# Two score slots of three PSUM banks each, side work on one bank, two early passes, and a plan picked among forty

## The chip, the cores and the metric

The kernel runs on one core of one Trainium2 chip. The metric is the device time of one execution in microseconds (us). Times are medians; a ratio is the mean time of one kernel's runs over the mean time of the other's of the same rounds, so it is not quite the ratio of the medians.

## The reference

Two transformer layers with shared weights over 2048 tokens of width 512: attention with 32 heads of 16 columns, then a feed-forward block of 1792 columns.

```python
x = x + _A_ref(_layernorm(x), A_wqkv, A_wo)     # attention, scores * Dh ** -0.5, softmax
x = x + _B_ref(_layernorm(x), B_w1, B_b1, B_w2, B_b2)   # gelu(x w1 + b1) w2 + b2
x = x + _A_ref(_layernorm(x), A_wqkv, A_wo)
x = x + _B_ref(_layernorm(x), B_w1, B_b1, B_w2, B_b2)
```

The attention asks for 2 x 32 x 2048 x 2048 exponentials. They set the time.

## The kernel before

The kernel contains a planner. It walks all the work in Python, keeps a clock for each engine from assumed costs and hand-over times, places each operation greedily by readiness and priority, and emits one fixed instruction stream per engine with semaphores. On the chip nothing is decided any more. A constant that only enters the planner's clocks changes no instruction's work, only the order, and through the order also how many cells go to which engine.

A *cell* is one PSUM bank of scores: 128 keys by 512 queries; there are 4096. ScalarE turns the cells of a *slot* into exponentials, three or two banks in one instruction (a *turn*). VectorE makes some of the cells with an integer approximation. Of the eight banks, 0 to 2 and 3 to 4 are the two slots, 5 collects the products with V, 6 and 7 are side banks, into which PE writes *side units*: pieces of the projections and of the feed-forward, each of some 16 matmuls or a longer sum, read out by VectorE or ScalarE. Between them PE also runs *filler* matmuls, whose results nobody uses. In the cuts below `...` marks what is left out, and the comments are mine.

```python
SLOTS = ((0, 1, 2), (3, 4))
PVB = 5
MISC = (6, 7)          # side work: projections, feed-forward, output projection
EARLY = 4              # early passes of the second query block of layer 1
LATENCY = {"pe": 0.20, "act": 0.10, "dve": 0.10, "pool": 0.15, "sp": 0.1}
MM = 0.2135            # the planner's length of a group of matmuls
```

VectorE gets its cells in two ways. *Attach*: beside a turn's scores PE writes one more cell into a free side bank. *Swap*: the third bank of a slot goes to VectorE, and ScalarE's turn is cut to two banks. Such a slot is refilled only after both have read it.

```python
def swap(self, op, start, cells, extra, free):
    if extra or self.lend == 2 or len(cells) < 3 or not (self.open or self.s.pools["du"]):
        return
    if self.s.clock["dve"] > start + SWAP:      # VectorE would not get to it soon
        return
    ...
    cells.pop()
    ...
    self.join(op, d, SLOTS[0][2], extra, free)

def route(self, name, b):                       # where a freed side bank goes
    ...
    return "misc" if q > (0 if b == MISC[0] else QUEUE if ... else RUSH) or b == MISC[0] else "dbank"

def exps(self):                                 # ScalarE
    ...
    src = self.bank(SLOTS[sl][0], n).rearrange("p (j q) -> p j q", j=n)
    yield _Op("act", 0.065 + 0.4267 * n, lambda e, src=src, dst=dst: e.activation(
        out=dst, in_=src, func=ACT.Exp, scale=0.25), reads=..., writes=...)
```

A VectorE cell costs PE four products with V (V itself and three scaled copies), a ScalarE cell one.

The softmax here doesn't subtract the row's maximum and nothing guards it: scores larger than these inputs give would overflow.

## Time and profile before

| | before |
|---|---|
| median (6 runs beside the changed kernel) | 1588.74 us (1587.05 to 1592.41) |
| span of the profiled run | 1587.3 us |
| busy ScalarE / PE / VectorE | 97% / 90% / 85% |

The prediction below shows the lines of this profile and how they are read. One quantity needs a word. A turn of n banks keeps ScalarE for n x 426.7 + 51 ns from its start to the start of the next, if the next one's scores are there. Whatever passes beyond that between two successive exponentials I call the *lateness* of the second. I sum it over all successive pairs of the trace. In the profile's own rows most of it is hidden in the exponentials' durations, since a record can begin before the one before it has ended (two-bank records last at least 1017 ns and follow each other at 904 ns); only the longer gaps appear as idle time.

### The profile page before, as it was taken

The numbers are of one execution on the slowest core, as the hardware profiler recorded it, in microseconds if no ns is written. First come the engines' busy times: TensorE is split into PE (matmuls) and PEld (weight loads), VectorE is DVE, ScalarE is ACT, GpSimd is POOL, SyncE is SP. The second block draws the span as 40 slices with busy tenths as digits, with TensorE's granted clock in tenths as the row PEclk, the third lists the DMA queues.
The fourth block names the chain that finished last, engine by engine and source line by source line (L and its number), as shares of the span: only waits on it lengthen the run. The fifth ranks groups of instructions, "written<-read, shape, count | busy, mean of one in ns | idle before, by whom it ended". The sixth has DMA issues, their size and how long they took to land.

```text
span 1587.3 us, 42896 instructions
## 1 busy us (share of the span) xinstructions
PE 1424.2 (90%) x18701; PEld 444.6 (28%) x18701; DVE 1352.0 (85%) x2564; ACT 1547.1 (97%) x1393; POOL 200.5 (13%) x250
## 2 busy tenths in 40 slices
PE   8998888899999898988989998888998889898988
PEld 3222222222222222222222222222222222333344
DVE  5689999888898889978788789899878988998984
ACT  7999999999999999999999999999999999999996
POOL 5200012001100201002120020122001000010000
PEclk9999999999999999999999999999999999999999
DMA  5100001241114311143111510001251105312520
GB/s 140 22 2 1 2 14 41 77 132 46 27 45 130 85 41 28 42 140 74 36 28 48 172 44 28 1 2 33 67 167 43 28 15 151 103 36 87 155 82 29
DMA packets 141767, 96.88 MB, mean 61 GB/s; under 512 B 36877, under 2 KB 141582, under 8 KB 141582
## 3 DMA queue, kind: packets, MB, share of 16 engines
q1 hardware_dynamic: 141582, 94.14, 21.2%
q8 instruction: 149, 2.44, 0.6%
q14 instruction: 36, 0.29, 0.1%
HBM read 84.41 MB, written 2.10 MB: 55 GB/s over the span
## 4 chain that ended last, share of the span: by engine, by line
ACT 67%; PE 29%; DVE 2%; POOL 1%; issue 1%; DMA 0%; ACTq 0%; POOLq 0%
ACT pt L1466 60%; PE ps L512 11%; PE ps L1137 9%; PE ps L1527 8%; ACT g L893 3%; ACT v L1466 2%; ACT kt L1466 1%; ACT q L1466 1%; DVE du L1283 1%; ACT L893 1%; ACT L1466 0%; DMA xf<-xln 0%; PE ps L1125 0%; POOL xln L602 0%; POOL rstd L588 0%
## 5 line engine op out<-in xcount | busy, mean ns | idle before, releaser
L1466 ACT ACTIVATE pt<-ps 128x1536 bf16<-128x1536 f32 (+2 forms) x1261 | 1384.2, 1246 | 15.2 <-PE ps L1137 10.3
L1137 PE MATMUL ps<-qp,kt 32*128 32x512 bf16 x4096 | 538.0, 385 | 140.8 <-ACT pt L1466 106.7
L1283 DVE TENSOR_SCALAR du<-ps 128x512 uint16<-128x512 f32 x711 | 479.7, 685 | 97.5 <-PE ps L1137 89.6
L1527 PE MATMUL ps<-pt,v 128*17 128x512 bf16 (+1 forms) x3368 | 433.8, 359 | 2.3 <-ACT pt L1466 0.8
L1527 PE MATMUL ps<-du,vc 128*17 128x512 bf16 (+1 forms) x2394 | 333.8, 358 | 2.7 <-DVE du L1346 1.4
L1137 PEld LDWEIGHTS ps<-qp,kt 32*128 32x128 bf16 x4096 | 140.6, 91 | 685.9 <-ACT pt L1466 304.2
L1346 DVE TENSOR_SCALAR du<-du 128x2048 uint16<-128x2048 uint16 x361 | 246.3, 687 | 2.5
L1085 POOL TENSOR_SCALAR qp<-q,mask 128x512 bf16<-128x512 bf16 (+1 forms) x91 | 66.3, 728 | 1013.8 <-PE ps L1137 1005.1
L512 PE MATMUL ps<-xf,wr 128*32 128x512 bf16 (+1 forms) x2400 | 170.8, 368 | 1.7 <-DMA xf<-xln 1.1
L1527 PE MATMUL ps<-du,v 128*17 128x512 bf16 (+1 forms) x798 | 154.7, 360 | 1.7 <-DVE xt L743 0.9
L1344 DVE TENSOR_SCALAR du<-du 128x1024 uint16<-128x1024 uint16 x361 | 150.5, 428 | 2.0
L1527 PEld LDWEIGHTS ps<-pt,v 128*17 128x17 bf16 x3368 | 111.8, 89 | 113.0 <-issue 72.9
L512 PE MATMUL ps<-wr,g 128*32 128x512 bf16 x1600 | 123.8, 384 | 5.5 <-ACT g L893 5.0
L1527 PEld LDWEIGHTS ps<-du,vc 128*17 128x17 bf16 x2394 | 92.5, 89 | 62.7 <-issue 27.5
L872 DVE TENSOR_SCALAR g<-ps,hb1t 128x512 bf16<-128x512 f32 (+1 forms) x112 | 79.8, 713 | 13.8 <-PE ps L512 12.9
L1527 PE MATMUL ps<-dh,vc 128*17 128x512 bf16 (+1 forms) x321 | 90.6, 358 | 0.0
L1283 DVE TENSOR_SCALAR dh<-ps 128x512 uint16<-128x512 f32 x96 | 65.8, 685 | 11.5 <-PE ps L1137 10.8
L1283 DVE TENSOR_SCALAR kt<-ps 128x512 uint16<-128x512 f32 x82 | 56.1, 684 | 20.7 <-PE ps L1137 19.9
L512 PEld LDWEIGHTS ps<-xf,wr 128*32 128x32 bf16 x2400 | 53.6, 95 | 61.5 <-issue 33.5
L602 POOL TENSOR_SCALAR xln<-x,rstd,nmr 128x512 bf16<-128x512 bf16 x58 | 58.2, 1008 | 33.3 <-DMA xf<-xln 23.2
L754 POOL TENSOR_TENSOR ott<-xt,rc 128x256 bf16<-128x256 f32 x42 | 29.5, 703 | 178.5 <-DVE rc L746 178.5
L1125 PE MATMUL ps<-vc 128*32 128x512 bf16 x476 | 50.9, 395 | 0.1
(93 smaller groups left out, 1185.2 us busy)
## 6 DMA issues: line engine op xcount, KB each, us to landing
wr<-in_B_w_dram SPq DMA_DIRECT2D x256, 256.0 KB, 2.9
wr<-in_A_wqkv_dram SPq DMA_DIRECT2D x24, 256.0 KB, 2.9
wr<-in_A_wo_dram SPq DMA_DIRECT2D x18, 256.0 KB, 2.9
out_dram<-x SPq DMA_DIRECT2D x16, 128.0 KB, 2.7
g<-in_A_wqkv_dram SPq DMA_DIRECT2D x3, 512.0 KB, 5.1
x<-in_A_x_dram SPq DMA_DIRECT2D x3, 512.0 KB, 8.0
q<-in_B_w_dram SPq DMA_DIRECT2D x3, 512.0 KB, 3.9
kt<-in_B_w_dram SPq DMA_DIRECT2D x4, 256.0 KB, 3.3
```

The source lines that it names most:

```text
L512: return [lambda e, a=a: e.matmul(out[32 * a:32 * a + 32, :], lhsT=lhsT[:, 32 * a:32 * a + 32], rhs=rhs, start=start, stop=stop, tile_posi ...
L602: yield _Op(eng, cost, lambda e: e.tensor_scalar(T["XLN"][:, x, :], T["X"][:, t, :], T["RSTD"][:, t:t + 1], T["NMR"][:, t:t + 1], op0=ALU. ...
L872: yield _Op("dve", 0.21 + n / 966, lambda e, fc=fc, pb=pb: e.tensor_scalar(T["G"][:, fc, q], pb, T["HB1T"][:, fc:fc + 1], None, op0=ALU.ad ...
L893: lambda e, g=g: e.activation(out=g, in_=g, func=ACT.Gelu_apprx_tanh), reads=gk, writes=gk, prio=2)
L1085: yield _Op("pool", 0.1 + 0.6 * w / 512, lambda e, s=s, q=q, i=i, t=t, w=w: e.tensor_scalar(T["QP"][:, s, w * i:w * i + w], q, T["MASK"][: ...
L1125: fns.append(lambda e, o=o, w=w, a=a, m=m: e.matmul(o, lhsT=w, rhs=rhs, start=start, stop=start, tile_position=(0, m * a)))
L1137: return (lambda e: e.matmul(o, lhsT=lhsT, rhs=rhs, start=True, stop=True, tile_position=(32 * a, 0)), ["K%d.%d.%d" % (l, gb, kt // 4), "Q ...
L1283: yield _Op("dve", 0.68, lambda e: e.tensor_scalar(u, self.bank(b), E_SCALE, E_BIAS, op0=ALU.mult, op1=ALU.add), reads=["B.%d" % b], write ...
L1344: yield _Op("dve", 0.08 + 0.14 * n, lambda e: e.tensor_scalar(U[:, 1, 0:n, :], U[:, 0, 0:n, :], SHIFT, None, op0=ALU.add), reads=key[0], w ...
L1346: yield _Op("dve", 0.08 + 0.28 * n, lambda e: e.tensor_scalar(U[:, 2:4, 0:n, :], U[:, 0:2, 0:n, :], 2 * SHIFT, None, op0=ALU.add), reads=k ...
L1466: yield _Op("act", 0.065 + 0.4267 * n, lambda e, src=src, dst=dst: e.activation(out=dst, in_=src, func=ACT.Exp, scale=0.25), reads=["B.%d" ...
L1527: op.fns.append(lambda e, o=o, lhsT=q[0][0][m], rhs=q[0][1][:, n * m:n * m + n], a=a, st=st, sp=sp: e.matmul(o, lhsT=lhsT, rhs=rhs, start= ...
```

## The change

The intent is to widen ScalarE's turns. The second slot gets a third bank once the first layer's side work allows; side work then has bank 7 alone; a swap may cut either slot; the second query block has two early passes in layer 1; small hand-overs and priorities are set; and the constants of the planner are those of the best of forty draws by its own simulation.

```diff
-PVB = 5
-MISC = (6, 7)
+WIDE = 5
+PVB = 6
+MISC = (7, 5)
-EARLY = 4
+EARLY = 2
-LATENCY = {"pe": 0.20, "act": 0.10, "dve": 0.10, "pool": 0.15, "sp": 0.1}
+LATENCY = {"pe": 0.20, "act": 0.103924, "dve": 0.090771, "pool": 0.142879, "sp": 0.1}
-MM = 0.2135
+MM = 0.21347002580386326
@@ norm: explicit hand-over of the buffers XT and OTT
+        yield ("acq", "xt")
...
+        if ts[0] == 0:
+            yield ("take", ("ott", o))
@@ post: priority of the last layer norm
-            yield ("spawn", self.ln(ts, xf, xk, LNP, last), LNP)
+            yield ("spawn", self.ln(ts, xf, xk, LNP, last), 0.2 if last else LNP)
@@ route
+        if b == WIDE:
+            return "wide"
@@ vcopies, when the scaled copies of V are made
             self.lend = 1
+            if WIDE in self.s.pools["misc"]:
+                self.s.pools["misc"].remove(WIDE)
+                self.s.pools["wide"].append(WIDE)
@@ swap, in both slots
-        f, r = self.score(c, self.s.tokens[("qp", c[0])], SLOTS[0][2])
+        f, r = self.score(c, self.s.tokens[("qp", c[0])], self.slots[sl][2])
...
-        self.join(op, d, SLOTS[0][2], extra, free)
+        self.join(op, d, self.slots[sl][2], extra, free)
@@ dfirst
-        if b in MISC:
+        if b == MISC[0]:
             yield ("rel", "dbank", b)
         else:
-            yield from self.slot_done(0)
+            yield from self.slot_done(0 if b < 3 else 1)
+    def widen(self):
+        yield ("acq", "wide")
+        self.slots[1].append(WIDE)
... (the other lines replace SLOTS by self.slots, set up the new pools, and adapt
     the banks for filler matmuls and one condition on the last block)
```

More of the change, by code (lines that the diff above doesn't have):

```diff
@@ L737, in norm @@
         xt = T["XT"]
+        gb, ts = self.heads(seg, g)
+        yield ("acq", "xt")
         if part:
@@ L747, in norm @@
                   reads=["XT"], writes=["RC"])
-        gb, ts = self.heads(seg, g)
         o = gb % 2
+        if ts[0] == 0:
+            yield ("take", ("ott", o))
         pool = g < 6 and seg[2] == 512
@@ L757, in norm @@
                 reads=["XT", "RC"], writes=["OTT.%d.%d" % (o, t)])
+        yield ("rel", "xt", 0)
         if ts[-1] == 1:
@@ L761, in norm @@
                       writes=["OTN.%d.%d" % (gb, t % 4) for t in self.tiles(seg)])
+            yield ("rel", "ott", o)
             yield ("give", ("otn", l, seg, gb))
@@ L900, in ytile @@
         last = NFC // 2 - 1
-        for p in range(1 if (l, seg) == (NL - 1, self.segs[l][-1]) else NFC // 2):
+        for p in range(1 if tail else NFC // 2):
             yield ("need", ("g", l, seg, p))
@@ L1053, in setup_attention @@
         self.lead = [min(pi for pi, p in enumerate(self.pas) if p[0] == l) for l in range(NL)]
+        self.slots = [list(x) for x in SLOTS]
         self.held, self.users = [len(x) for x in SLOTS], [0] * len(SLOTS)
@@ L1093, in free @@
         src = self.source()
-        for b in (6, 7, 0, 1, 2, 3, 4, 5) if src else ():
+        for b in (7, 5, 0, 1, 2, 3, 4) if src else ():
             k = "B.%d" % b
@@ L1190, in join, with swap @@
         self.nd += 1
-    def swap(self, op, start, cells, extra, free):
+    def swap(self, op, start, cells, extra, free, sl):
         if extra or self.lend == 2 or len(cells) < 3 or not (self.open or self.s.pools["du"]):
@@ L1241, in scores @@
             cells = []
-            for _ in SLOTS[sl]:
+            for _ in self.slots[sl]:
                 c = self.next_act()
@@ L1248, in scores @@
                 break
-            work = list(zip(cells, SLOTS[sl]))
+            work = list(zip(cells, self.slots[sl]))
             fns, reads, writes, free, extra = [], [], [], [], []
@@ L1261, in scores @@
             op = _Op("pe", MM, fns, reads=reads, writes=writes, mode="S", slack=max(SLACK, ahead - LATE))
-            op.late = lambda op, start: (self.attach(op, start, cells, extra, free), self.swap(op, start, cells, extra, free))
+            op.late = lambda op, start, sl=sl, cells=cells, extra=extra, free=free: (self.attach(op, start, cells, extra, free), self.swap(op, start, cells, extra, free, sl))
             yield op
             self.held[sl] = len(cells)
-            self.users[sl] = 1 + any(e[1] in SLOTS[sl] for e in extra)
+            self.users[sl] = 1 + any(e[1] in self.slots[sl] for e in extra)
             for d, b, pair, j in extra:
@@ L1463, in exps @@
                 yield ("take", ("pt", r))
-            src = self.bank(SLOTS[sl][0], n).rearrange("p (j q) -> p j q", j=n)
+            src = self.bank(self.slots[sl][0], n).rearrange("p (j q) -> p j q", j=n)
             dst = self.unit(run)
@@ L1467, in exps @@
                 out=dst, in_=src, func=ACT.Exp, scale=0.25),
-                reads=["B.%d" % b for b in SLOTS[sl][:n]], writes=[k for r in run for k in self.pkeys(r)])
+                reads=["B.%d" % b for b in self.slots[sl][:n]], writes=[k for r in run for k in self.pkeys(r)])
             for r, (pi, kt, a) in zip(run, cells):
@@ L1478, in exps @@
             yield ("take", ("s", sl))
-            for b in SLOTS[sl]:
+            for b in self.slots[sl]:
                 yield ("rel", "misc", b)
@@ L1564, in run @@
         s.pool("dbank", [])
+        s.pool("wide", [])
+        s.pool("xt", [0])
+        s.pool("ott", [0, 1])
         s.route = self.route
@@ L1586, in run @@
         s.spawn(self.solo(), 4)
+        s.spawn(self.widen(), 4)
         for c in range(self.NQ):
```

## The prediction

> **What bounds the kernel now.** I read the page's first table, then its chain of work that ended last, then the groups by form on ScalarE and VectorE, then the waits, then the stretches of 40 us.
>
> ```profile
> PE 1424.2 (90%) x18701; PEld 444.6 (28%) x18701; DVE 1352.0 (85%) x2564; ACT 1547.1 (97%) x1393; POOL 200.5 (13%) x250
> ACT 67%; PE 29%; DVE 2%; POOL 1%; issue 1%; DMA 0%; ACTq 0%; POOLq 0%
> ```
>
> ScalarE is busy for 97% of the span and carries two thirds of the chain. Of its 40 us outside work, some 8 lie before 40 us and 15 after 1560 us, where the last feed-forward runs with no attention left. So between the ends ScalarE hardly ever stands still, and time is won there by giving it less to do, or by making its instructions follow each other more tightly.
>
> ```profile
> L1466 ACT ACTIVATE pt<-ps 128x1024 bf16<-128x1024 f32 x769 | 798.2, 1080 | 7.4 <-PE ps L1137 6.0
> L1466 ACT ACTIVATE pt<-ps 128x1536 bf16<-128x1536 f32 x491 | 740.2, 1507 | 7.8 <-PE ps L1137 4.2 <-PE ps L1527 1.3
> L1466 ACT ACTIVATE v<-ps 128x1536 bf16<-128x1536 f32 x18 | 26.6, 1477 | 0.2
> L1466 ACT ACTIVATE kt<-ps 128x1536 bf16<-128x1536 f32 x17 | 25.2, 1481 | 0.4 <-PE ps L1137 0.4
> L1283 DVE TENSOR_SCALAR du<-ps 128x512 uint16<-128x512 f32 x711 | 479.7, 685 | 97.5 <-PE ps L1137 89.6
> L1346 DVE TENSOR_SCALAR du<-du 128x2048 uint16<-128x2048 uint16 x350 | 241.2, 693 | 2.5
> L1344 DVE TENSOR_SCALAR du<-du 128x1024 uint16<-128x1024 uint16 x350 | 147.9, 433 | 2.0
> ```
>
> A cell of scores is one bank, 128 keys by 512 queries; there are 4096. ScalarE takes exponentials of three banks (1536 columns) or two (1024) at once, from the two slots in turn. Over all output names I count 540 instructions of three banks, 793 of two, one of one: 1334 instructions, 3207 cells, 2.40 cells each. VectorE makes the other 711 + 96 + 82 = 889 cells by its integer form; all its exponential groups sum to 1114 us, 1.253 us a cell, so its other work is 1352 - 1114 = 238 us. Equal slot turns would give 667 of each width; 540 means that 127 three-bank turns were cut to two by a swap that hands the third bank to VectorE. Then 762 of VectorE's cells came through the separate banks 6 and 7.
>
> From start to start the trace has a median of 904 ns after a two-bank exponential and 1331 ns after a three-bank one. The difference, 427 ns, is 512 columns at 1.2 GHz; what is left over either is 51 ns. Durations in the groups are longer because successive instructions overlap, so I use starts. Over all 1321 successive pairs of exponentials the excess over 427 ns a cell sums to 112 us: 67 us is the 51 ns floor, 45 us is lateness, and nearly all the lateness (41 us) follows two-bank instructions (mean excess over the floor 48 to 62 ns, against 7 ns after three banks).
>
> ```profile
> DVE du L1283 <- PE ps L1137: 89.6, 180, 3.1
> DVE kt L1283 <- PE ps L1137: 19.9, 22, 4.5
> DVE dh L1283 <- PE ps L1137: 10.8, 26, 2.1
> ```
>
> VectorE, which could relieve ScalarE, stands 120 us waiting for score cells, half of its 235 us of idle time. The stretches show where:
>
> ```profile
> 160.00:200.00 40.00, 32.41 (x364) 8.74 (x363) 37.77 (x74) 39.99 (x36) 3.02 (x4) 1.00 0.01 2
> 680.00:720.00 40.00, 35.78 (x470) 11.00 (x470) 27.63 (x50) 39.88 (x32) 1.34 (x3) 1.00 0.53 154
> 880.00:920.00 40.00, 36.72 (x483) 10.88 (x485) 30.17 (x53) 39.80 (x37) 1.39 (x2) 1.00 0.55 158
> ```
>
> The columns after the stretch's length are busy PE, weight loads, VectorE, ScalarE, GpSimd, then clock and DMA. With no side work (160 to 200 us) VectorE is 94% busy. In the second feed-forward product (high DMA) it falls to 69 to 75%, while ScalarE stays full: both side banks are held for long sums, and cells reach VectorE only by a swap in the one three-bank slot.
>
> **What the Trainium skill says.** "Perfetto Trace Analysis", section "Optimizing Scalar/DVE Operations", gives about 51 ns of access overhead per ScalarE instruction on PSUM and advises grouping when the engine is saturated. The start-to-start medians above agree to the nanosecond. The same page, "Identifying the Most-Contended Engine", takes occupancy as a fair measure for ScalarE and VectorE but not for matmuls; so 90% of PE is no proof that PE is close behind, and PE also runs 476 + 468 matmuls (L1125) of pure filler, 95 us of busy records. "PSUM — Partial Sum Buffer", section "PSUM bank collisions raise a hardware error", asks for semaphores by bank: a three-bank slot of which one bank goes to VectorE may only be refilled when both readers are done. This trace shows the cost of such waits as the lateness above.
>
> **The change part by part.**
>
> 1. Slots (0,1,2) and (3,4) become (0,1,2) and (3,4,5) once the first layer's projections are nearly done. Bank 5 is a side bank until then, so the opening keeps two side banks and 3 + 2. If no turn were swapped, 3207 cells would take 1069 instructions, a gain of 265 x 51 ns = 13.5 us. But every swapped turn drops back to two.
>
> 2. Afterwards side work has bank 7 alone, and VectorE's separate cells may use it only when no side unit holds it. A projection, first-product or output-projection unit is 0.98 us of matmuls (chain rows) plus a VectorE read of 0.69 to 0.75 us and two hand-overs: I estimate 2.5 us as interleaved. Four wo, fourteen first-product and twelve projection units make 75 us per segment of 192 us; four long sums of sixty matmuls at about 7 us make 28. So bank 7 is held some 54% of the time. It fits, but about half of the cells that came by separate banks must now come by swap.
>
> 3. Swaps are allowed in both slots. With about 450 of the cells swapped and 470 attached, ScalarE's width is about 2.6: from 3 x N = 3175 + 450 comes N = 1208 and a width of 2.63; I take 2.6, N = 1221. Saved: 113 x 51 ns = 5.8 us.
>
> 4. More cells for VectorE: up to one swap offer per turn instead of one per two turns, just where both side banks were busy. I assume that a third of its 120 us of score waits is recovered: 40 us / 1.253 us = 32 cells, 921 in all. Each spares ScalarE 0.427 us: 13.7 us. The ceiling is 1024 cells (4 of 16 key tiles), and the first 75 us offer hardly any, so a large leap is not possible.
>
> 5. Lateness: about 60% of turns now have three banks. 733 x 7 ns + 488 x 60 ns = 34 us against 45. Swapped slots wait for VectorE as well, so I take 9 us less, not 11.
>
> 6. Two early passes instead of four: two partial copies (0.69 us) and two adds (0.68 us) fewer, 2.7 us of VectorE, about 2 cells, under 1 us of time. It leaves 480 instead of 576 cells to cover the last segment's side work of layer 0, which is paced over 450. It should just fit.
>
> 7. The transposed-output buffers get explicit hand-over and the last normalization a higher priority. The tail of 26 us after the last exponential is one chain through PE (L512, 14 us in one piece); I give it 1 us. Changed latency constants alter no instruction; they shuffle the plan and, with a pick of forty by the planner's own clock, promise perhaps more than the chip will give. I count nothing.
>
> 8. Cost: side units can no longer overlap one's product with another's evacuation. Where a chain of them sets when a segment's next stage starts, ScalarE may run dry: 4 us, mainly at the layer boundary (1040 to 1160 us, where ScalarE already lacks 3.4 us in two stretches).
>
> Sum: -5.8 - 13.7 - 9 - 1 - 1 + 4 = -26.5 us, counted as -26: 1589.7 - 26 = **1564 us**, 1.6% less.
>
> **The rivals.**
>
> A. The swaps eat the width. If side work holds bank 7 more than I think, nearly all VectorE cells come by swap: N = (3207 + 889)/3 = 1365, more instructions than now, so no width gain; only lateness and the tail move: about 1580 to 1588. For it: 127 swaps now, concentrated where side work runs. Against: 120 to 200 us, with no side work, has 58 cells and no swaps, and bank 7 alone can serve one attached cell per 1.33 us turn.
>
> B. VectorE saturates. A third of the missing 120 us is a guess; if two thirds come back, 64 cells, 27 us instead of 13.7, and with thicker slots 1545 to 1550. For it: ScalarE and VectorE would both run over 90%. Against: several waits come with only single buffers of probability units, and PE order is static.
>
> C. Side work becomes the bound: one bank serializes, the layer boundary and feed-forwards slip, ScalarE shows gaps of several us. That makes 1590 to 1610. Against: 54% hold; for: the long sums keep the bank for 7 us while normalized tiles wait.
>
> **How the range follows.** The three uncertain terms are cells (0 to 65: 0 to 28 us), width plus lateness (0 to 25 us), and side work (0 to 20 us against). They are partly opposed, so eight times in ten I expect 1543 to 1584 us. Over 2% faster means below about 1558.5: 0.37. Within 2%: 0.59. Slower: 0.04, since the static plan can see a jam in advance and bank 7's load has room.
>
> **What would show it.** Step 1 and 3: the count of exponentials falls from 1334 to about 1220 (1365 would be rival A), with three-bank forms the majority. Step 4: cells at the first integer step rise from 889 to about 920 and VectorE's waits for scores fall from 120 to about 80 us; busy in the second-product stretches over 31 of 40. Step 5: the median 904 and 1331 ns stay, the sum of lateness falls to about 36 us. Step 8: ScalarE idle between 40 and 1560 us stays under 20 us; long gaps released by PE L512 or by the transposed load of XF would be rival C. If VectorE makes fewer than 889 cells, the prediction is wrong at step 4 and each missing cell costs 0.43 us.

## The result, and the profile after

The changed kernel took 1587.81 us (1585.58 to 1592.9, 6 runs) against 1588.74 us: ratio 0.9994, 95% interval 0.9975 to 1.0014. That is the same, where 26 us less was forecast, and it lies outside the stated range.

The page's first table of the changed kernel, and its chain:

```profile
PE 1414.1 (89%) x18817; PEld 443.9 (28%) x18817; DVE 1368.3 (86%) x2582; ACT 1538.2 (97%) x1346; POOL 195.3 (12%) x248
ACT 60%; PE 34%; DVE 3%; issue 1%; POOL 1%; DMA 0%; POOLq 0%; ACTq 0%
```

ScalarE's busy time fell by only 9 us, and the chain shows who took over: PE went from 29% to 34% of it. The groups by form on ScalarE, and on VectorE:

```profile
L1482 ACT ACTIVATE pt<-ps 128x1536 bf16<-128x1536 f32 x568 | 810.9, 1534 | 10.3 <-PE ps L1149 6.0 <-PE ps L1543 3.7
L1482 ACT ACTIVATE pt<-ps 128x1024 bf16<-128x1024 f32 x654 | 661.5, 1075 | 13.0 <-PE ps L1149 10.1
```

```profile
L1295 DVE TENSOR_SCALAR du<-ps 128x512 uint16<-128x512 f32 x726 | 493.6, 686 | 93.3 <-PE ps L1149 86.0
L1295 DVE TENSOR_SCALAR dh<-ps 128x512 uint16<-128x512 f32 x94 | 64.5, 686 | 10.3 <-PE ps L1149 9.4
L1295 DVE TENSOR_SCALAR kt<-ps 128x512 uint16<-128x512 f32 x85 | 58.2, 685 | 12.7 <-PE ps L1149 11.8
```

Over all output names there are 618 turns of three banks, 668 of two, one of one: 1287. Two-bank turns are still the majority, although both slots have three banks. VectorE makes 726 + 94 + 85 = 905 cells, 16 more. Its waits for scores (86.0 + 11.8 + 9.4 us) are 107 us, against 120. The same three stretches as in the prediction, columns as there:

```profile
160.00:200.00 40.00, 32.34 (x378) 8.55 (x377) 35.20 (x65) 40.00 (x34) 3.38 (x5) 0.96 0.00 1
680.00:720.00 40.00, 36.79 (x457) 10.74 (x445) 32.79 (x61) 38.35 (x33) 1.63 (x2) 0.96 0.38 113
880.00:920.00 40.00, 38.39 (x502) 11.17 (x499) 34.87 (x64) 39.37 (x39) 1.39 (x2) 1.00 0.54 159
```

In the second-product stretches VectorE rose as hoped, from 27.63 to 32.79 and from 30.17 to 34.87 us, and there ScalarE lost 1.5 and 0.4 us of its busy time. (Part of the 1.5 us is the clock, which the sixth column gives as 0.96; see below.) Without side work (160 to 200 us) VectorE fell from 37.77 to 35.20.

Matching the traces with the program's order, which is possible because the counts of instructions on ScalarE, VectorE and PE agree exactly, I can tell by which bank each VectorE cell came and who held bank 7:

| | before | after |
|---|---|---|
| cells by swap | 124 (bank 2) | 654 (341 bank 2, 313 bank 5) |
| cells by a side bank | 765 (583 bank 7, 182 bank 6) | 251 (bank 7) |
| side bank held by side work | 765 us (bank 6), 89 us (bank 7) | 819 us (bank 7) |
| pairs of two-bank turns in succession, their mean distance | 252, 966 ns | 364, 985 ns |
| lateness | 45.0 us | 52.8 us |
| of it, of turns that overlap with a stretch at half clock | 5.1 us | 10.6 us |

So in the new structure 514 fewer cells come by a side bank and 530 more by a swap: 16 more in all.

The account closes. 16 cells at 427 ns are 6.8 us off ScalarE, 47 instructions at 51 ns are 2.4 us, lateness is 7.8 us more: together -1.4 us. The spans differ by -1.5 us (1587.3 to 1585.8).

But the account mixes in the clock. The trace has stretches, most of them of 3.41 us, in which PE was granted half its clock: four before (17.1 us in all), nine after (30.7 us). Of the 7.8 us of added lateness 5.5 us belong to turns that overlap with them; at full clock lateness rose only from 39.8 to 42.1 us. The mean granted clock of an execution goes with its time: the six runs of the changed kernel lie between 1592.9 us at 0.985 and 1585.58 us at 0.994, 0.8 us for each 0.001, and the 43 runs of the kernel before that stand beside the experiments have the same slope. Those have a mean clock of 0.993, the six of the changed kernel 0.990. At equal clock the changed kernel would be some 3 us faster, by an estimate from these numbers, and still far from 26. Whether the change itself lowers the clock, no run shows.

What a late turn looks like, in the timeline of ScalarE and of PE in the changed kernel (start, length, what, idle before it):

```profile
1228.82 2.14 ACT L1482 ACTIVATE pt<-ps 128x1024 bf16<-128x1024 f32 x2
1231.88 1.02 ACT L1482 ACTIVATE pt<-ps 128x1024 bf16<-128x1024 f32 x1 [0.91 <-PE ps L1149]
```

```profile
1229.51 0.39 PE L1149 MATMUL ps<-qp,kt 32*128 32x512 bf16 x3
...
1229.83 0.59 PE L1543 MATMUL ps<-pt,v 128*17 128x512 bf16 x3
...
1230.44 1.07 PE L513 MATMUL ps<-xf,wr 128*32 128x512 bf16 x16
1231.44 0.39 PE L1149 MATMUL ps<-qp,kt 32*128 32x512 bf16 x3
```

```profile
1229.63 0.75 DVE L878 TENSOR_SCALAR g<-ps,hb1t 128x512 bf16<-128x512 f32 x1 [0.34 <-PE ps L513]
1230.29 1.28 DVE L1295 TENSOR_SCALAR du<-ps 128x512 uint16<-128x512 f32 x2
```

ScalarE does two cut turns in a row and is through at 1230.96. Its next turn begins at 1231.88, 1.03 us late. Two things make it late. Its slot is free only at 1230.97, when VectorE has read the swapped bank (the first of the two L1295), after reading a side bank (L878). And its scores (L1149) start only at 1231.44, behind a full side unit of sixteen matmuls (L513) that PE's fixed order puts in front. By the shortest way that the traces show from a free slot to its exponential (0.48 us, see e9), the first makes 0.6 us of the delay and the second 0.4 us. Of the ten latest turns of this trace six overlap with, or closely follow, a stretch at half clock.

### The profile page after: what moved, and what is told of

It reads as the page before. It is cut to its first block, busy times and chain, and to the rows that moved or that the text cites. A ratio compares the mean times of both kernels' runs of the same rounds, so it can differ in the third digit from the quotient of the medians.

```text
span 1585.8 us, 43201 instructions
## 1 busy us (share of the span) xinstructions
PE 1414.1 (89%) x18817; PEld 443.9 (28%) x18817; DVE 1368.3 (86%) x2582; ACT 1538.2 (97%) x1346; POOL 195.3 (12%) x248
## 3 DMA queue, kind: packets, MB, share of 16 engines
q1 hardware_dynamic: 141582, 94.14, 21.1%
## 4 chain that ended last, share of the span: by engine, by line
ACT 60%; PE 34%; DVE 3%; issue 1%; POOL 1%; DMA 0%; POOLq 0%; ACTq 0%
ACT pt L1482 53%; PE ps L513 13%; PE ps L1543 11%; PE ps L1149 10%; ACT g L899 3%; ACT kt L1482 2%; ACT q L1482 1%; DVE du L1295 1%; ACT v L1482 1%; ACT L1482 1%; ACT L899 1%; DMA xf<-xln 0%; DVE g L878 0%; PE ps L1137 0%; DVE du L1356 0%
## 5 line engine op out<-in xcount | busy, mean ns | idle before, releaser
L1482 ACT ACTIVATE pt<-ps 128x1024 bf16<-128x1024 f32 (+1 forms) x1223 | 1384.3, 1288 | 23.3 <-PE ps L1149 16.1
L1149 PE MATMUL ps<-qp,kt 32*128 32x512 bf16 x4096 | 519.5, 386 | 150.2 <-ACT pt L1482 108.6
L1295 DVE TENSOR_SCALAR du<-ps 128x512 uint16<-128x512 f32 x726 | 493.6, 686 | 93.3 <-PE ps L1149 86.0
L1543 PE MATMUL ps<-pt,v 128*17 128x512 bf16 (+1 forms) x3379 | 454.7, 361 | 2.8 <-ACT pt L1482 0.9
L1543 PE MATMUL ps<-du,vc 128*17 128x512 bf16 (+1 forms) x2445 | 329.7, 359 | 0.2
L1149 PEld LDWEIGHTS ps<-qp,kt 32*128 32x128 bf16 x4096 | 137.2, 91 | 680.9 <-ACT pt L1482 263.5
L1358 DVE TENSOR_SCALAR du<-du 128x2048 uint16<-128x2048 uint16 x364 | 251.4, 693 | 2.6
L513 PE MATMUL ps<-xf,wr 128*32 128x512 bf16 (+1 forms) x2400 | 170.2, 368 | 1.5 <-DVE g L878 0.9
L1356 DVE TENSOR_SCALAR du<-du 128x1024 uint16<-128x1024 uint16 x364 | 154.0, 433 | 2.6
L1543 PEld LDWEIGHTS ps<-pt,v 128*17 128x17 bf16 x3379 | 117.1, 89 | 122.5 <-issue 80.2
L1543 PE MATMUL ps<-du,v 128*17 128x512 bf16 (+1 forms) x815 | 149.6, 362 | 1.4 <-DVE xt L746 0.6
L513 PE MATMUL ps<-wr,g 128*32 128x512 bf16 x1600 | 124.1, 390 | 3.4 <-ACT g L899 1.7
L878 DVE TENSOR_SCALAR g<-ps,hb1t 128x512 bf16<-128x512 f32 (+1 forms) x112 | 79.9, 714 | 16.7 <-PE ps L513 15.0
L1295 DVE TENSOR_SCALAR dh<-ps 128x512 uint16<-128x512 f32 x94 | 64.5, 686 | 10.3 <-PE ps L1149 9.4
L513 PEld LDWEIGHTS ps<-xf,wr 128*32 128x32 bf16 x2400 | 51.7, 95 | 62.4 <-issue 35.9
L1295 DVE TENSOR_SCALAR kt<-ps 128x512 uint16<-128x512 f32 x85 | 58.2, 685 | 12.7 <-PE ps L1149 11.8
L1137 PE MATMUL ps<-vc,zero 128*17 128x512 bf16 x644 | 57.6, 387 | 0.7 <-POOL vc L1077 0.7
```

The source lines that it names most:

```text
L513: return [lambda e, a=a: e.matmul(out[32 * a:32 * a + 32, :], lhsT=lhsT[:, 32 * a:32 * a + 32], rhs=rhs, start=start, stop=stop, tile_posi ...
L878: yield _Op("dve", 0.21 + n / 966, lambda e, fc=fc, pb=pb: e.tensor_scalar(T["G"][:, fc, q], pb, T["HB1T"][:, fc:fc + 1], None, op0=ALU.ad ...
L1137: fns.append(lambda e, o=o, w=w, a=a, m=m: e.matmul(o, lhsT=w, rhs=rhs, start=start, stop=start, tile_position=(0, m * a)))
L1149: return (lambda e: e.matmul(o, lhsT=lhsT, rhs=rhs, start=True, stop=True, tile_position=(32 * a, 0)), ["K%d.%d.%d" % (l, gb, kt // 4), "Q ...
L1295: yield _Op("dve", 0.68, lambda e: e.tensor_scalar(u, self.bank(b), E_SCALE, E_BIAS, op0=ALU.mult, op1=ALU.add), reads=["B.%d" % b], write ...
L1356: yield _Op("dve", 0.08 + 0.14 * n, lambda e: e.tensor_scalar(U[:, 1, 0:n, :], U[:, 0, 0:n, :], SHIFT, None, op0=ALU.add), reads=key[0], w ...
```

## The experiments

All have five rounds or three beside the kernel before on the same chip. The table has every run; lateness (in brackets that of turns overlapping with half clock), exponentials (N) and VectorE cells (D) are from the profiled execution, the ratio is to the kernel before.

| run | median us | ratio | span us | N | D | lateness us (at half clock) |
|---|---|---|---|---|---|---|
| before | 1588.74 | 1 | 1587.3 | 1334 | 889 | 45.0 (5.1) |
| after | 1587.81 | 0.9994 | 1585.8 | 1287 | 905 | 52.8 (10.6) |
| e1 round constants | 1595.17 | 1.0038 | 1595.0 | 1290 | 917 | 66.8 (10.2) |
| e2 before, no swap | 1605.54 | 1.0107 | 1603.7 | 1300 | 847 | 42.2 (5.8) |
| e3 after, no swap | 1747.85 | 1.0998 | 1742.4 | 1209 | 484 | 30.1 (8.4) |
| e4 swap in first slot only | 1644.48 | 1.0357 | 1642.1 | 1252 | 726 | 33.9 (4.7) |
| e5 late widening | 1589.65 | 0.9998 | 1587.8 | 1293 | 911 | 57.0 (8.0) |
| e7 after, other draw | 1603.2 | 1.0082 | 1601.4 | 1289 | 916 | 70.4 (16.8) |
| e8 four early passes | 1596.0 | 1.0048 | 1598.1 | 1290 | 904 | 61.5 (14.2) |
| e9 two products fewer | 1580.88 | 0.9943 | 1576.6 | 1277 | 923 | 51.4 (7.8) |
| e10 before, bad draw | 1610.14 | 1.0131 | 1613.2 | 1331 | 884 | 61.4 (10.3) |
| e11 before, best draw | 1583.8 | 0.9969 | 1582.4 | 1342 | 901 | 44.5 (7.0) |
| e12 late widening, best draw | 1583.6 | 0.9967 | 1583.6 | 1294 | 914 | 53.9 (10.5) |
| e13 no two cuts in a row | 1631.54 | 1.0272 | 1626.3 | 1261 | 783 | 38.2 (6.8) |
| d1 old / new | 1595.85 / 1597.85 | 1.0038 / 1.0042 | 1593.9 / 1597.3 | 1346 / 1284 | 885 / 893 | 46.6 / 56.0 (4.0 / 9.5) |
| d2 old / new | 1605.95 / 1600.1 | 1.0103 / 1.0064 | 1605.0 / 1599.5 | 1337 / 1290 | 890 / 900 | 54.9 / 58.4 (13.9 / 11.7) |
| d3 old / new | 1599.43 / 1594.9 | 1.0072 / 1.0034 | 1596.1 / 1595.6 | 1332 / 1290 | 877 / 909 | 44.6 / 64.0 (5.9 / 7.2) |

The theories after the result: (A) the bank given to the second slot was VectorE's own supply, and swaps only buy it back; (L, C) the cut turns make ScalarE late; (S) the single side bank makes it late; (P) what is left is the draw of the plan.

### e2 and e3: what the bank was worth

Edit in both structures: no swap.

```diff
-        if self.s.clock["dve"] > start + SWAP:
+        if True:
             return
```

> The kernel before without the swap of a slot's third bank to VectorE: VectorE's cells come by the separate banks 6 and 7 alone. The built program has 847 VectorE cells and 1300 exponentials. 42 cells less by 0.427 us make 18 us more, 34 instructions fewer by 51 ns make 2 us less: 1600 to 1608 us. Shows what separate banks alone carry with two of them.

> The changed kernel without any swap: six score banks always of three, VectorE's cells by bank 7 alone, which side work shares. The built program has 484 VectorE cells and 1209 exponentials, 1194 of three banks. Theory A (the bank given to the second slot was VectorE's supply, and each cell lost costs ScalarE 0.427 us): 421 cells fewer than the changed kernel make 180 us, 78 instructions fewer give back 4 us: about 1755 to 1770 us, with ScalarE 98% busy. Theory W (wider turns themselves are worth much because they take away lateness): well below that, under 1740 us. In both the lateness after three-bank turns shows what the wide turns are worth by themselves.

Measured 1605.54 and 1747.85 us. The first page row of e3 shows what is left of VectorE:

```profile
PE 1411.6 (81%) x18199; PEld 430.5 (25%) x18199; DVE 941.2 (54%) x1711; ACT 1703.4 (98%) x1268; POOL 186.9 (11%) x248
```

Theory A holds. With separate banks alone the old structure still makes 847 VectorE cells, the new one 484: giving the bank away costs 363 cells, 155 us of ScalarE at 427 ns each, and ScalarE is 98% busy while VectorE idles. The time fell between my two expectations for e3, because lateness also fell, by 22.7 us against the changed kernel; the account by spans is 421 x 0.427 - 78 x 0.051 - 22.7 = 153 us, measured 156.6. So turns that all have three banks are late by less, 25 ns each on average against 41 ns in the changed kernel, but not by the 7 ns that step 5 carried over from the three-bank turns of the kernel before; and one does not get such turns and VectorE's cells together.

### e4: the swap in one slot only

```diff
-        if extra or self.lend == 2 or len(cells) < 3 or not (self.open or self.s.pools["du"]):
+        if sl or extra or self.lend == 2 or len(cells) < 3 or not (self.open or self.s.pools["du"]):
```

> The changed kernel with the swap allowed in the first slot only, as the kernel before had it. The built program has 726 VectorE cells, 1252 exponentials. Theory A: 179 cells fewer than in the changed kernel make 76 us, 35 instructions fewer save 2 us: about 1655 to 1662 us. If the second slot's swap were only a replacement for attached cells (rival), cells would hardly fall; the count already speaks against it, and the time should follow the count.

Measured 1644.48 us, 11 us under the expected range; the expected sum had no term for lateness. By spans: from e4 to the changed kernel the second slot's swap brings 179 cells (76.4 us), costs 35 instructions (1.8 us) and 18.9 us of lateness; net 55.7 us, measured 56.3. A quarter of what these cells give is handed back as late turns. From e3 to e4 the first slot's swap brings 242 cells for 3.8 us of lateness. So a cell costs 16 ns of lateness in the first step and 106 ns in the second; at full clock, 31 and 73 ns. It costs more once both slots are cut.

### e13: no two cut turns in succession

```diff
-        if extra or self.lend == 2 or len(cells) < 3 or ...
+        if self.held[1 - sl] < 3 or extra or self.lend == 2 or len(cells) < 3 or ...
```

> The changed kernel, in which a slot may be cut to two banks by a swap only if the other slot's last turn had three, so that two short turns never follow each other after the opening. Side work keeps its single bank. 783 VectorE cells, 1261 exponentials. Theory C (short turns in succession make the lateness, not the single side bank): the sum of lateness falls from 53 to 30 to 40 us, and the time is 1588 + 52 (122 cells) - 1 (26 instructions) - 16 (lateness) = about 1623 us. Theory S (the single side bank makes it): lateness stays above 48 us and the time is about 1637 us.

Lateness fell to 38.2 us (at full clock from 42.1 to 31.4 us) with the single side bank kept, as theory C says and against theory S. The time, 1631.54 us, is halfway between the two expectations: cells (52.1 us), instructions (1.3) and lateness (14.6) explain 36.2 of the 40.5 us between the spans, and 4.3 us are not explained. e3 and e4 speak the same way: one side bank, lateness 30.1 and 33.9 us. The three kernels also have fewer VectorE cells and so less work for PE in a given time, so this shows that the single side bank alone does not bring the lateness, not that it has no part in it.

### e9: less work for PE

The wanted proof that PE's load makes the late turns: of the four products of each VectorE cell only two are made. The result is wrong.

```diff
-            for i in range(4):
+            for i in range(2):
...
-                                         ("du", du) if i == 3 else None, i == 3, kt))
+                                         ("du", du) if i == 1 else None, i == 1, kt))
```

> Wrong result on purpose: of the four products with V that each VectorE cell costs PE (one with V, three with scaled copies) only the first two are made; ScalarE's and VectorE's instructions for a cell stay as they are. It takes about 2 x 900 of some 6800 products off PE. Theory L (in a cut turn PE has 0.90 us for scores, four products for VectorE's cell and the side work, and comes late): lateness falls from 53 us to 35 or less and the time to 1565 to 1577 us. Rival (the late turns come from waiting for VectorE's read of the swapped bank or from the one side bank, not from PE's load): the lateness stays above 45 us and the time above 1580 us.

Measured 1580.88 us and a lateness of 51.4 us. This goes to the rival.

```profile
PE 1332.5 (85%) x17217; PEld 407.8 (26%) x17217; DVE 1378.1 (87%) x2622; ACT 1527.4 (97%) x1336; POOL 202.4 (13%) x248
```

PE's busy time fell by 82 us, though the planner put 440 more filler matmuls into the room. The gain came from 18 more VectorE cells (7.7 us) and 10 instructions fewer. To see what the late turns wait for I asked of each turn over 25 ns late whether its slot was free in time. In the traces at least 0.48 us pass from the end of the last reader of the banks that a turn's scores fill, through the scores, to the start of the exponential. Where the banks were free early enough for a turn to be on time, PE's order made it late. In the changed kernel this holds for 45.7 of 49.7 us; 2.7 us wait for VectorE's read of such a bank, 1.2 us for ScalarE's. In the kernel before it is 33.8 of 41.7 us, in e9 36.7 of 48.2. PE did not stand idle meanwhile: of the 95.3 us between a free slot and its first score it was busy for 94.5, with products with V (53.9), side units (36.2) and hardly any filler (2.1). Sorted by what PE did in between, lateness in us, at full clock in brackets (the small rest falls under neither column):

| | with a side unit | with products alone | slot free too late |
|---|---|---|---|
| before / after | 13.6 / 22.0 (12.1 / 15.7) | 16.4 / 20.3 | 7.9 / 3.9 |
| e9 | 21.1 (17.4) | 10.3 | 11.4 |
| d1 old / new | 11.9 / 20.0 (10.6 / 16.1) | 19.0 / 20.4 | 10.4 / 7.1 |
| d2 old / new | 14.8 / 26.8 (12.7 / 19.6) | 17.0 / 17.4 | 10.5 / 5.8 |
| d3 old / new | 12.0 / 16.2 (11.3 / 16.1) | 18.9 / 24.2 | 5.8 / 8.6 |
| e3, e4, e13 | 13.8, 9.6, 10.3 (12.1, 9.6, 8.5) | 5.6, 10.5, 15.4 | 0.5, 1.9, 1.2 |

Halving the products halved what products alone bring (20.3 to 10.3 us), as theory L has it; what a side unit brings stayed, and waits for a slot rose by 7.5 us. So theory L falls in the form I gave it, PE's total load. What sets the new structure apart in all four pairs is the turns with a side unit in between. In e3, e4 and e13, which have the single side bank but no two cut turns in succession, that part is as small as in the old structure. So the traces point to the two together, short turns in succession and a side unit between them, and not to the single side bank by itself. No run changes only that.

### e5: widening after the projections

```diff
+        for c in range(self.NQ):
+            for kind in "KVQ":
+                for i in range(4):
+                    yield ("need", (kind, 0, 4 * c + i if kind == "V" else i, c))
         ... (bank 5 leaves the side pools only here)
         yield ("acq", "wide")
         self.slots[1].append(WIDE)
```

> The changed kernel, but bank 5 goes to the second slot only after the last of the first layer's projections (all 48 queries, keys and values tiles) has been read out; in the changed kernel it goes when the copies of V are made, with 11 projections still to come, and ScalarE then stands or is late for 4.7 us between 80 and 120 us. Theory O (the opening is short of side banks): that stretch's lateness falls to about 1 us. Since every plan falls differently, the total may move by some us either way from other stretches; the built program has 911 VectorE cells and 1293 exponentials, against 905 and 1287. Time expected: 1584 to 1592 us. If the lateness between 80 and 120 us stays, the single side bank there was not the cause.

The stretch from 80 to 120 us (columns as above), in the changed kernel and then in e5:

```profile
80.00:120.00 40.00, 34.60 (x453) 10.40 (x450) 32.66 (x60) 35.77 (x33) 2.63 (x4) 1.00 0.01 2
```

```profile
80.00:120.00 40.00, 36.76 (x447) 10.30 (x445) 34.63 (x64) 39.19 (x38) 3.30 (x4) 1.00 0.01 2
```

ScalarE gets its 3.4 us back (39.19 us busy, the very number of the kernel before), and the lateness there falls from 5.3 to 1.8 us, so the early hand-over of bank 5 did cost that. The total did not move (1589.65 us): the rest of the plan fell differently, with two waits of 2.0 and 2.6 us for VectorE's partial sums near 1030 and 1044 us. A local repair is worth its local gain only if the plan behind it stays.

### e8: four early passes

```diff
-EARLY = 2
+EARLY = 4
```

> The changed kernel with four early passes of the second query block as before, not two. VectorE has two partial copies and two adds more (2.7 us). 904 VectorE cells, 1290 exponentials. If two early passes were worth something by themselves: slower than the changed kernel by more than the spread that one reordering of the plan gives (4 us). If not (my expectation): 1590 to 1598 us, a loss of the size of a redrawn plan, with the lost time as lateness spread over the whole span and not in the stretch where the second layer begins (960 to 1160 us).

Measured 1596.0 us. The size was as expected, the place was not: I had written that the loss would not lie where the second layer begins. From 960 to 1160 us, first the changed kernel, then e8:

```profile
960.00:1160.00 200.00, 173.42 (x2159) 50.20 (x2156) 176.72 (x329) 196.66 (x168) 26.85 (x33) 0.99 0.21 61
```

```profile
960.00:1160.00 200.00, 164.49 (x1938) 47.06 (x1937) 177.78 (x329) 190.67 (x158) 29.27 (x34) 0.97 0.09 24
```

ScalarE is busy for 6 us less just there. But the clock differs too (0.99 and 0.97): of the 5.8 us that lateness rises in this stretch, 3.6 us belong to turns at half clock, in one execution. So the loss of 8 us stands, for this plan, and its place does not. The kernel before has four and loses only 0.7 us against the changed kernel in that stretch (195.97 us busy), so whether two are better in general one draw cannot say.

### e1 and e7: the pick, in the new structure

e1 takes back the constants (0.10, 0.10, 0.15, 0.2135); e7 has another draw within 10% on three latencies and 0.03% on the matmul.

> The changed kernel with the latency and matmul constants of the kernel before (0.10, 0.10, 0.15, 0.2135): everything of the change but the pick of one plan among forty. The constants enter no instruction, only the order in which the plan places them. Theory P (the pick carries what little gain there is; the structure as such is worth about nothing): slower than the changed kernel by 4 to 10 us, so 1592 to 1598 us, slightly slower than the kernel before. Theory B (the structure is worth something and the pick is cosmetic): within 2 us of 1587.8. The built program has 1290 exponentials (600 of three banks) and 917 VectorE cells, so by cells and instructions alone it should even be 5 us faster than the changed kernel; if it is slower, the time lies in late score turns.

> The changed kernel with another draw of the four constants that only order the plan (up to 10% either way on three latencies, 0.03% on the matmul's length), the worst by the planner of forty that I drew. 916 VectorE cells and 1289 exponentials: by cells it should be 5 us faster than the changed kernel. Theory P (the pick is worth real time, through the late score turns): 1600 to 1610 us, with the sum of lateness 15 to 25 us above the changed kernel's 53 us. If the planner's order of plans does not hold on the chip: within 4 us of 1588.

Measured 1595.17 and 1603.2 us: 7 and 15 us slower than the changed kernel, with 12 and 11 *more* VectorE cells, and with 14 and 18 us more lateness (14 and 11 us at full clock). Theory P holds here: everything of the change but the pick is 0.4% slower than the kernel before (ratio 1.0038, 1.0025 to 1.005).

### e10 and e11: the pick, in the old structure

> The kernel before with other ordering constants, the worst by the planner of 934 draws: 884 VectorE cells and 1331 exponentials instead of 889 and 1334, so by cells and instructions 2 us slower. Theory P (the order of the plan alone is worth as much as the whole change was hoped to give, in the old structure too): 1605 to 1618 us, the loss being lateness of ScalarE's turns. If the old structure is robust and only the new one depends on the draw: under 1598 us.

> The kernel before, structure untouched, with the best by the planner of 934 draws of the ordering constants: 901 VectorE cells, 1342 exponentials (8 more). Theory P: if a pick among draws is what can be had, the old structure gets as much from it as the new one: 1579 to 1587 us, at or below the changed kernel. Against P: slower than 1589.

Measured 1610.14 and 1583.8 us. The old structure is just as sensitive. In e10 one single wait, ended by a product with V (L1527), carries much of it:

```profile
1524.82 5.97 ACT L1466 ACTIVATE pt<-ps 128x1536 bf16<-128x1536 f32 x5 [10.13 <-PE ps L1527]
```

ScalarE stands for 10 us there. And e11, with not a line of the change's structure, is faster than the changed kernel by 4 us.

### d1 to d3: both structures under the same constants

What was open after that was whether the structure is worth something apart from the draw. Three sets of constants, the first three of a generator, went into both. The only edits are LATENCY and MM, for d1 for example 0.0927, 0.1069, 0.1579 and 0.21347.

> First paired draw, the structure before: 885 VectorE cells, 1346 exponentials. Expected 1595 to 1603 us. If the structure of the change is worth nothing, the changed structure under the same constants is within 5 us of it; if it is worth what I predicted, 20 us or more faster.

> First paired draw, the structure of the change: 893 VectorE cells (8 more, 3.4 us), 1284 exponentials (62 fewer, 3.2 us). If lateness did not change, 6.6 us faster than the structure before under the same constants; with 8 us more lateness, as between the two kernels, equal within 5 us. Expected 1595 to 1603 us.

> Second paired draw, the structure before: 890 VectorE cells, 1337 exponentials. Expected 1597 to 1607 us.

> Second paired draw, the structure of the change: 900 VectorE cells (10 more, 4.3 us), 1290 exponentials (47 fewer, 2.4 us): 6.7 us faster if lateness stayed, equal within 5 us if it rises by 8. Expected 1594 to 1604 us.

> Third paired draw, the structure before: 877 VectorE cells, 1332 exponentials. Expected 1594 to 1604 us.

> Third paired draw, the structure of the change: 909 VectorE cells (32 more, 13.7 us), 1290 exponentials (42 fewer, 2.1 us). This is the very gain in cells that my prediction put in its sum: if lateness stayed, 16 us faster than the structure before under the same constants. If added cells come back as lateness, within 5 us of it. Expected 1594 to 1604 us.

The pairs differ by +2.0, -5.9 and -4.5 us in medians (new minus old), a mean of -2.8 us. The mean clock of the runs differs within the pairs (0.996 and 0.989, 0.987 and 0.989, 0.989 and 0.994); with 0.8 us for each 0.001 I estimate -3.6, -3.9 and -0.3 us at equal clock, a mean of -2.6. From three pairs, the structure is worth about 0.2%, if anything; 20 us is excluded. The third pair is the most telling:

```profile
PE 1435.0 (90%) x18776; PEld 446.2 (28%) x18776; DVE 1345.0 (84%) x2538; ACT 1550.9 (97%) x1391; POOL 202.7 (13%) x250
```

```profile
PE 1413.2 (89%) x18752; PEld 444.5 (28%) x18752; DVE 1376.6 (86%) x2592; ACT 1538.8 (96%) x1349; POOL 202.2 (13%) x248
```

Here the new structure gives exactly the 32 more cells of my sum, and ScalarE's busy time falls by 12 us. Lateness rises by 19.4 us, and 4.5 us are left in the medians, where the clock favours the new structure, and 0.5 us in the profiled spans, at the same clock of 0.991. (The account by spans would give 3.6 us lost; 4 us are not explained.) Lateness rose in all three pairs: 9.4, 3.5, 19.4 us, at full clock 4.0, 5.7 and 18.1 us.

### e12: the best version

The late widening of e5, a lateness allowance of 0.85 us instead of 0.7, and the best of 934 draws.

> The best version that the runs so far point to: the changed kernel with bank 5 handed over after the first layer's projections, the lateness allowance 0.85 us instead of 0.7, and the best by the planner of 934 draws. 914 VectorE cells, 1294 exponentials: against the changed kernel 9 cells more (3.8 us less), 7 instructions more, and lateness between 80 and 120 us about 3 us less. 1576 to 1584 us, faster than both kernels, but by less than 1%.

Measured 1583.6 us, ratio 0.9967 (0.9954 to 0.9979): faster than both kernels by 0.3%, and no faster than e11, the old structure with its best draw. Both are correct.

## Why the prediction was wrong, point by point

Two steps failed. Step 5 cost the sum most: it made lateness depend on a turn's width alone and gave 9 us less, where 7.8 us more were measured (2.3 us more at full clock); most late turns find PE busy with other work between their free slot and their scores (e9). And the reading behind steps 2 and 4 was wrong, that VectorE stands idle in the second-product stretches because both side banks are held. By the matched trace of the kernel before, side work holds bank 6 there (36 of 40 us from 680 to 720 us) and bank 7 not at all; 17 of VectorE's 19 cells came by bank 7, one by a swap. Bank 7 was VectorE's own feed. The change gave it to side work, and the swaps bought the cells back by cutting the turns that were to become wide.

- **The bound, and its price list.** Right: the 51 ns floor and 427 ns a bank stayed, ScalarE stayed at 97%, and with them the accounts above close within some 4 us.
- **Step 2, the hold of bank 7.** The 54% were right (819 us of some 1500), by luck: short units held the bank for 2.16 us and not 2.5, long sums for 9.9 and not 7. What I made of it was wrong: I took 470 cells to come by bank 7 in its free time; 251 did. A free bank is used only if it is free when a turn's scores are issued.
- **Step 3, width.** Mis-sized: 654 swaps instead of 450, width 2.48 instead of 2.6, 1287 exponentials instead of 1221; 2.4 us instead of 5.8. This is half of rival A, whose window of time (1580 to 1588 us) also held the result, though not its count of 1365.
- **Step 4, cells.** Mis-sized: 16 more instead of 32, 6.8 us instead of 13.7. VectorE gained in the second-product stretches as argued and lost where there is no side work, because there it had lived on its own banks. Its waits for scores fell to 107 us, not 80.
- **Step 5, lateness.** Wrong in sign, and the largest miss: +7.8 us instead of -9, or +2.3 us at full clock. I took the lateness of a turn to depend on its width alone (60 and 7 ns) and the number of cut turns to fall to 40%. It fell only from 59% to 52%, more of them now follow each other (364 pairs, 252 before), and each such pair became later (81 ns instead of 62 over the floor). The turns after three-bank ones became later too: by 17 ns on average instead of 7. I had also set PE aside ("90% of PE is no proof that PE is close behind") and put lateness down to waits for both readers of a slot. In the kernel before only 7.9 of 41.7 us wait for a reader of the slot; most late turns find PE busy with something else (e9).
- **Step 6, early passes.** I gave under 1 us; e8 is 8 us slower than the changed kernel, but in one plan, which a redrawn order can bring alone. It did not decide the sum.
- **Step 7, the pick.** I counted nothing for it. On the chip it is worth 7 us against the round constants (e1) and 15 against a bad draw (e7). Without it the change loses. The 1 us for the tail did not come: after the last exponential 26.5 us pass in both kernels.
- **Step 8, side work.** The 4 us came about in size, by coincidence, but elsewhere: 3.4 us in the opening, where step 1 had assumed the projections to be nearly done. ScalarE's idle time between 40 and 1560 us rose from 16.7 to 24.2 us, over the 20 us given as the sign.

Small slips in the prediction's figures: 124 turns were cut and not 127, so 765 cells came by side banks and not 762; 2% below 1589.7 us is 1557.9 and not 1558.5.

The sum as measured: -2.4 (3), -6.8 (4), +7.8 (5, with 8 and the opening in it) = -1.4 us.

What stays open: how much of the late turns a better order could avoid at the same number of cells, whether the single side bank has a part in them (the kernels that lower lateness also lower VectorE's cells), and whether a plan itself sets how often the clock is halved.

## What to carry to other kernels

When a buffer is moved from one engine's supply to another's, count what the giver did with it before counting what the receiver gains: here the two side banks had fed VectorE 765 cells, the one that was left fed it 251, and the swaps that made up for it cut the very turns that were to become wide. Where a planner fixes the order, compare structures under several identical draws; a single pair of plans differs by as much as this change was hoped to bring. And look at the granted clock before explaining a few microseconds: here 0.001 of it went with 0.8 us.

## What the Trainium skill lacked or had wrong

- "Perfetto Trace Analysis", section "Optimizing Scalar/DVE Operations": the 51 ns of ScalarE on PSUM are right, from start to start, for two banks (904 ns) and three (1331 ns). The page does not say that the next exponential must have its scores for that to hold; the mean over all pairs in the kernel before is 85 ns.
- "ScalarE: Activation LUTs", section "What ACT_TABLE_LOAD costs", gives about 2.66 us for a switch of tables, 1.38 of it a drain. Here the load takes 1.28 us, as the page says, but only 1.31 us pass in all: in the changed kernel the last exponential ends at 1559.34, the load stands at 1559.36, and the Gelu begins at 1560.65 us.
- The same section has back-to-back ACTIVATEs overlap by about 93 ns. Exponentials from PSUM with two banks have records of at least 1017 ns at a distance of 904 ns, an overlap of 113 ns.
- No page gives the shortest way from a reader that frees a PSUM slot, through PE's scores, to the next exponential: at least 0.48 us in these traces, more than half of a two-bank turn.
- No page warns that a fixed order of much the same work is a source of variation of its own: 1583.8 to 1610.14 us in the old structure, 1587.81 to 1603.2 us in the new one.
